# One output tile moved across the chunk border, and two product steps set next to each other, in the expert loop of an attention, experts and tanh-shrink kernel

## The chip, the cores and the metric

The kernel runs on one core of a Trainium2 chip. The metric is device time in microseconds of one execution; the median of several executions counts, and the profile shows one further execution with every instruction in time. TensorE (PE) multiplies and writes PSUM, its weight loads (PEld) are listed apart; VectorE (DVE) and ScalarE (ACT) read PSUM and write SBUF; GpSimd (POOL) works on SBUF; SyncE (SP) issues most of the DMAs.

## What is computed

```python
def _attn_ref(q, k, v, p):                  # batch 4, heads 8, seq 576, head_dim 64, 32 packed rows
    p_packed = sm_attn(p, k, v)             # softmax attention of the packed rows
    return sm_attn(q, p_packed, p_packed)   # and of all tokens over the packed rows

x = attn_out.transpose(0, 2, 1, 3).reshape(2304, 512)
p = domain_probs / (domain_probs.sum(-1, keepdims=True) + 1e-09)
for e in range(4):                          # experts, w1[e] 512x1024, w2[e] 1024x512
    h = np.maximum(x @ w1[e], 0.0)
    out += p[:, e:e + 1] * (h @ w2[e])
h = out @ w_in                              # 512x2048
return (h - np.tanh(h)) @ w_out             # 2048x512
```

## The kernel before, in words

The program has three parts: attention (to about 95 us), the expert loop (to about 650 us) and the tanh-shrink layers (to the end). The change lies in the expert loop.

The tokens are worked in two halves (`p` = 0 and 1), each of two batch elements of 576 tokens (1152 tokens, nine tiles of 128). The four experts' hidden columns are cut into eight chunks `c` of 512. For one half and one chunk the loop does these things, each named by a letter in a string of tokens that `run` reads in order:

- `g` (`up_prod`, L660): the first layer of one batch element. It is a fast block multiplication with seven products in four steps, `g<c><p><element><step>`. Steps 0 to 2 have two products of six matmuls with 288 columns each, into the PSUM tiles X and Z; step 3 has one, into X. Matmuls go on accumulating into X and Z over the steps, and between them the other engines read the intermediate sums: `kept` (ACT copies a sum out) and `done` (L686: DVE adds a kept sum to the one in PSUM at L687, then `split_h`, L610, writes the relu of it as a high part by ACT, L612, and a low part by DVE, L613). In step 2 `done` reads X first, then Z. In step 3 X gets its last product and is split.
- `d` (`down`, L723): the second layer for one tile of 128 tokens, 12 matmuls of 512 columns into a PSUM tile `yps` (two buffers), which DVE then adds to the output tile `x2` with the expert's probability (L746). Tiles 0 to 3 hold the first element only, tile 4 both, tiles 5 to 8 the second.
- `y` and `p` (`pack_pair`, `pack_held`): the next chunk's packed weights, 32 short matmuls into `wps` and the sums that the block multiplication needs (`pack_sums`, L584: four ACT and seven DVE operations).
- `a` (`stage`): loads of the next chunk's weights; `b` (`prep`): their split into high and low parts, done in the first half only and reloaded in the second; `k` (`save_w2`): storing the split ones.
- `_` (`background`, L971): one step of decoding the last layers' weights from 64-bit words, spread over DVE, ACT, POOL and DMAs. Its instructions are queued behind the last recorded DVE and ACT instruction of the steps before (`last`).

The loop runs a pair of strings per chunk: EVEN (the first element's products, with the tiles 4 to 8 of the chunk ahead) and ODD (the second element's products, with the tiles 0 to 3 of this chunk). EVEN0 and ODD0 are the same with fewer background calls; they serve the chunks 3 to 6 of the first half. The first chunks and the turn between the halves have strings of their own, as has the last chunk of the second half. So the pair of strings runs 12 times (L1091, L1092), eight times as ODD and four as ODD0.

PE and SP take their instructions in the order in which the strings issue them. DVE and ACT are ordered by a planner, which simulates the program and takes what is ready. A PSUM tile that a matmul wants to write while another engine still has to read it makes the matmul's weight load wait on a semaphore.

The order on PE around the place in question, before: g03, y, d7, d8 (both of the chunk ahead), g10, d0, g11, d1, g12, d2, g13, d3, and then the next chunk's g00. X and Z (`hpx`, `hpz`) and the first tile of `y` share two PSUM buffers of one pool.

Of the kernel before, what the change touches and what calls it, by code (L numbers as in the profile page):

```python
# [80 lines left out]
)  # L81

ODD = (
    "g%(c)d%(p)d10 a1%(e)d0 _ d%(c)d%(p)d0 _ g%(c)d%(p)d11 b%(e)d0 _ d%(c)d%(p)d1 a1%(e)d1 _ g%(c)d%(p)d12 "
    "d%(c)d%(p)d2 g%(c)d%(p)d13 p%(e)d%(q)d _ d%(c)d%(p)d3 b%(e)d1 _ "
)

EVEN0 = (
# [2 lines left out]
)  # L91

ODD0 = (
    "g%(c)d%(p)d10 a1%(e)d0 _ d%(c)d%(p)d0 _ g%(c)d%(p)d11 b%(e)d0 d%(c)d%(p)d1 a1%(e)d1 _ g%(c)d%(p)d12 "
    "d%(c)d%(p)d2 g%(c)d%(p)d13 p%(e)d%(q)d d%(c)d%(p)d3 b%(e)d1 _ "
)

LASTA = (
# [1238 lines left out]
```

## Time and profile before

| | |
|---|---|
| median of 3 runs | 1053.56 us (1053.47 to 1054.77) |
| the profiled execution | 1053.99 us, of it 1052.2 us span |
| PE busy | 1043.1 us (99%) |
| PE weight loads busy | 897.9 us (85%) |
| DVE busy | 883.1 us (84%) |
| ACT busy | 622.6 us (59%) |
| POOL busy | 162.1 us (15%) |
| granted PE clock | full speed in all slices |

The span is the time from the first to the last instruction in the profile; the execution's own time is a little longer. Matmuls overlap in the pipeline, so the durations of single ones add up to more than the time; distances between starts are the better measure. The end of a group of matmuls is read here as the start of the next matmul. "Idle before" in brackets is the idle time of an engine ahead of the instruction, and what ended it.

### The profile page before, as it was taken

To read this page: it belongs to the slowest core of one execution; us is meant where nothing else is said; L and a number is where in the kernel's file an instruction comes from. 1 tells how busy PE (TensorE), PEld (TensorE's weight loads), DVE (VectorE), ACT (ScalarE), POOL (GpSimd) and SP (SyncE) were. 2 spreads that over 40 slices of the span, in tenths; PEclk is the share of its full clock that TensorE was granted. 3 is DMA by queue.
4 is the path that set the end of the run, shared out by engine and by line. 5 is a ranking of instruction groups with operands and counts; after the bars stand their busy time and mean duration, and the time that the engine had idled before them with its cause. 6 is when DMAs were issued, how large, how long until landed. Compare 5 with 4: busy or idle time off the path is not lost.

```text
span 1052.2 us, 16516 instructions
## 1 busy us (share of the span) xinstructions
PE 1043.1 (99%) x6347; PEld 897.9 (85%) x6347; DVE 883.1 (84%) x1355; ACT 622.6 (59%) x986; POOL 162.1 (15%) x134
## 2 busy tenths in 40 slices
PE   8999999999999999999999999999999999999998
PEld 6778888788888888888888888999899899899897
DVE  5878988988986776988897986799988899988877
ACT  4555554545454455554554544578877778777775
POOL 1000032322323202424242431000000000000000
PEclk9999999999999999999999999999999999999999
DMA  9756435545654455375356254353555554564442
GB/s 337 246 188 212 171 127 187 190 161 160 220 197 134 160 175 167 139 250 180 107 205 243 83 215 164 137 214 142 195 219 186 205 202 143 205 259 162 189 170 81
DMA packets 57871, 192.75 MB, mean 183 GB/s; under 512 B 6464, under 2 KB 9024, under 8 KB 54720
## 3 DMA queue, kind: packets, MB, share of 16 engines
q1 hardware_dynamic: 57504, 191.49, 51.3%
q8 instruction: 50, 0.82, 0.3%
q14 instruction: 29, 0.24, 0.1%
q10 hardware_dynamic: 288, 0.20, 0.1%
HBM read 144.74 MB, written 46.92 MB: 182 GB/s over the span
## 4 chain that ended last, share of the span: by engine, by line
PE 96%; DVE 2%; ACT 1%; DMA 1%; issue 0%; SPq 0%; DVEq 0%
PE yps L733 37%; PE ops L1156 19%; PE h3ps L927 17%; PE hpx L676 8%; PE hpz L676 6%; PE wps L578 3%; PE hps L628 2%; PE pv L313 1%; PE qsc L335 1%; PE sc L252 1%; DMA kt<-in_kT_dram 1%; PE xps L842 0%; PE qtp L392 0%; PE tp L295 0%; PE xps L802 0%
## 5 line engine op out<-in xcount | busy, mean ns | idle before, releaser
L1156 PE MATMUL ops<-wo,gh 128*128 128x512 f32 x574 | 177.6, 390 | 0.0
L1156 PEld LDWEIGHTS ops<-wo,gh 128*128 128x128 f32 x574 | 107.1, 188 | 20.5
L746 DVE SCALAR_TENSOR_TENSOR x<-yps,pn,x 128x512 f32<-128x512 f32 x126 | 93.9, 746 | 31.2 <-PE yps L733 30.5
L733 PE MATMUL yps<-w2h,h0h 128*128 128x512 f32 x288 | 115.8, 402 | 0.0
L733 PE MATMUL yps<-w2h,h0l 128*128 128x512 f32 x288 | 113.4, 394 | 0.1
L733 PE MATMUL yps<-w2h,h1h 128*128 128x512 f32 x288 | 113.1, 393 | 0.0
L733 PE MATMUL yps<-w2l,h0h 128*128 128x512 f32 x288 | 112.9, 392 | 0.0
L1156 PE MATMUL ops<-wo,gl 128*128 128x512 f32 x287 | 112.6, 392 | 0.0
L733 PE MATMUL yps<-w2h,h1l 128*128 128x512 f32 x288 | 112.5, 391 | 0.0
L733 PE MATMUL yps<-w2l,h1h 128*128 128x512 f32 x288 | 112.2, 389 | 0.0
L927 PE MATMUL h3ps<-xh,wg 128*128 128x384 f32 x384 | 103.6, 336 | 0.0
L937 ACT ACTIVATE h<-h3ps 128x384 f32<-128x384 f32 x96 | 46.9, 490 | 70.6 <-PE h3ps L927 70.6
L449 POOL TENSOR_TENSOR fo<-fo,f 128x512 f32<-128x512 f32 x32 | 43.6, 1364 | 271.9 <-DVE f L445 184.4
L676 PE MATMUL hpx<-th,wp 128*128 128x288 f32 x336 | 80.7, 295 | 0.0
L733 PEld LDWEIGHTS yps<-w2h,h0h 128*128 128x128 f32 x288 | 54.0, 187 | 20.8 <-issue 10.9
L927 PEld LDWEIGHTS h3ps<-xh,wg 128*128 128x128 f32 x384 | 69.9, 188 | 0.7
L943 DVE TENSOR_TENSOR h<-h3ps,h 128x384 f32<-128x384 f32 x72 | 39.9, 554 | 30.6 <-PE h3ps L927 26.2
L733 PEld LDWEIGHTS yps<-w2h,h0l 128*128 128x128 f32 x288 | 54.0, 188 | 12.8 <-DVE h0l L613 0.6
L733 PEld LDWEIGHTS yps<-w2h,h1l 128*128 128x128 f32 x288 | 54.1, 188 | 12.3
L733 PEld LDWEIGHTS yps<-w2l,h1h 128*128 128x128 f32 x288 | 54.1, 188 | 12.1
L927 PE MATMUL h3ps<-xl,wg 128*128 128x384 f32 x192 | 64.3, 335 | 0.0
L733 PEld LDWEIGHTS yps<-w2h,h1h 128*128 128x128 f32 x288 | 54.1, 188 | 11.6
(192 smaller groups left out, 2591.0 us busy)
## 6 DMA issues: line engine op xcount, KB each, us to landing
wg<-wing SPq DMA_DIRECT2D x24, 1792.0 KB, 7.4
wraw<-in_w_dram SPq DMA_DIRECT2D x48, 512.0 KB, 6.4
wo<-wout SPq DMA_DIRECT2D x48, 512.0 KB, 8.7
w2s<-w2h SPq DMA_DIRECT2D x16, 512.0 KB, 3.9
w2s<-w2l SPq DMA_DIRECT2D x16, 512.0 KB, 4.3
f<-in_win_dram SPq DMA_DIRECT2D x16, 512.0 KB, 5.6
f<-in_wout_dram SPq DMA_DIRECT2D x16, 512.0 KB, 4.3
wing<-f SPq DMA_DIRECT2D x32, 256.0 KB, 4.5
```

The source lines that it names most:

```text
L252: nc.tensor.matmul(out=sc[64 * jj:64 * jj + 64, h, 0:288], lhsT=pbd[:, 4 * b + j, :], rhs=kv_k[b][j][:, 288 * h:288 * h + 288],)
L313: nc.tensor.matmul(out=pv[64 * h:64 * h + 64, jj, :], lhsT=kv_v[b][c][:, 128 * j + 64 * h:128 * j + 64 * h + 64], rhs=a1t[:, c, k0:k0 + 32 ...
L449: nc.gpsimd.tensor_tensor(out=lf, in0=lf, in1=st[:, :, 1].bitcast(F32), op=ALU.mult)
L578: nc.tensor.matmul(out=ps[32 * j:32 * j + 32, r, :], lhsT=ppbd[p][d, bi, j, 32 * r:32 * r + 32], rhs=raw[0, c, j // 2][d, j % 2, :],)
L628: nc.tensor.matmul(out=ps[:, ff, 0:n], lhsT=a[c, p, bi][:, g, c0:c0 + 128], rhs=x[p][:, g, t0:t0 + n], start=(k == 0), stop=(k == 5),)
L676: nc.tensor.matmul(out=ps[:, ff, 0:HB], lhsT=W[a][:, slot, c0], rhs=x[b], start=(start and k == 0), stop=(stop and k == 2), skip_group_che ...
L733: nc.tensor.matmul(out=ps, lhsT=a[:, ff, o:o + 128], rhs=w[c, fp][:, ff], start=(k == 0), stop=(k == 11),)
L746: last[0] = nc.vector.scalar_tensor_tensor(out=x2[tt], in0=ps, scalar=pn[:, tt, e:e + 1], in1=x2[tt], op0=ALU.mult, op1=ALU.add,).ins
L927: nc.tensor.matmul(out=ps, lhsT=wg[n][:, a, slot, 128 * kk:128 * kk + 128], rhs=x[c][b][kk] if isinstance(x[c][b], list) else x[c][b][:, k ...
L937: nc.scalar.activation(out=hs[n][a][b], in_=xz[n]["XZ".index(i)], func=ACTF.Copy)
L943: nc.vector.tensor_tensor(out=t, in0=xz[n]["XZ".index(i)], in1=t, op=ALU.add)
L1156: nc.tensor.matmul(out=ps, lhsT=a, rhs=wo[n][ff][:, w], start=(i == 0 and ff == 0 and k == 0), stop=(i == NG - 1 and ff == 1 and k == 2), ...
```

## The change

Only the two strings ODD and ODD0 are changed; no instruction is added or removed. d0 (the first output tile of this chunk) moves ahead of g10, next to d8 (the last one of the chunk ahead). g12 moves behind d2, so that g12 and g13 (third and fourth product steps of the second element) are next to each other. d1 comes between g10 and g11 and d2 between g11 and g12. The background calls keep their number and shift by a place: the first now stands ahead of d0, and of the later ones in ODD one more stands ahead of g11.

```diff
 ODD = (
-    "g%(c)d%(p)d10 a1%(e)d0 _ d%(c)d%(p)d0 _ g%(c)d%(p)d11 b%(e)d0 _ d%(c)d%(p)d1 a1%(e)d1 _ g%(c)d%(p)d12 "
-    "d%(c)d%(p)d2 g%(c)d%(p)d13 p%(e)d%(q)d _ d%(c)d%(p)d3 b%(e)d1 _ "
+    "_ d%(c)d%(p)d0 g%(c)d%(p)d10 a1%(e)d0 _ d%(c)d%(p)d1 _ g%(c)d%(p)d11 b%(e)d0 a1%(e)d1 _ "
+    "d%(c)d%(p)d2 g%(c)d%(p)d12 g%(c)d%(p)d13 p%(e)d%(q)d _ d%(c)d%(p)d3 b%(e)d1 _ "
 )
...
 ODD0 = (
-    "g%(c)d%(p)d10 a1%(e)d0 _ d%(c)d%(p)d0 _ g%(c)d%(p)d11 b%(e)d0 d%(c)d%(p)d1 a1%(e)d1 _ g%(c)d%(p)d12 "
-    "d%(c)d%(p)d2 g%(c)d%(p)d13 p%(e)d%(q)d d%(c)d%(p)d3 b%(e)d1 _ "
+    "_ d%(c)d%(p)d0 g%(c)d%(p)d10 a1%(e)d0 d%(c)d%(p)d1 _ g%(c)d%(p)d11 b%(e)d0 a1%(e)d1 _ "
+    "d%(c)d%(p)d2 g%(c)d%(p)d12 g%(c)d%(p)d13 p%(e)d%(q)d d%(c)d%(p)d3 b%(e)d1 _ "
 )
```

The order on PE after it: g03, y, d7, d8, d0, g10, d1, g11, d2, g12, g13, d3, then g00.

## Rows read from the trace of the kernel before

**Rows 1.** The page, busy us (share of the span) and instructions of each engine.
```profile
PE 1043.1 (99%) x6347; PEld 897.9 (85%) x6347; DVE 883.1 (84%) x1355; ACT 622.6 (59%) x986; POOL 162.1 (15%) x134
```

**Rows 2.** The page, the chain that ended last, share of span by engine.
```profile
PE 96%; DVE 2%; ACT 1%; DMA 1%; issue 0%; SPq 0%; DVEq 0%
```

**Rows 3.** Stretches: length, then busy us (instructions) by engine, granted clock, DMA share, GB/s.
```profile
133.45:171.45 38.00, 38.00 (x233) 31.91 (x225) 33.61 (x53) 19.45 (x33) 13.41 (x10) 1.00 0.51 160
200.00:215.00 15.00, 13.60 (x91) 10.33 (x90) 14.01 (x20) 6.82 (x12) 7.62 (x5) 1.00 0.44 141
```

**Rows 4.** The chain in order of time, merged: start us, us, what.
```profile
518.50 5.68 PE yps L733 x24
525.76 2.77 PE yps L733 x12
...
556.50 5.68 PE yps L733 x24
...
614.02 5.48 PE yps L733 x24
```

**Rows 5.** Waits of PE, whole span: us in total, times, longest.
```profile
PE wps L578 <- DVE u L687: 1.4, 1, 1.4
...
PE hps L628 <- DVE a2l L396: 0.2, 1, 0.2
```

**Rows 6.** Timeline of PE at 209: start us, us, instruction, idle before.
```profile
209.04 0.66 PE L578 MATMUL wps<-wraw,ppbd 64*32 64x512 f32 x8 [1.40 <-DVE u L687]
```

**Rows 7.** Timeline at 600: accumulation of d7, first matmul behind d8.
```profile
599.51 0.74 DVE L746 SCALAR_TENSOR_TENSOR x<-yps,pn,x 128x512 f32<-128x512 f32 x1
...
600.02 0.29 PE L676 MATMUL hpx<-a2h,wp 128*128 128x288 f32 x1
```

**Rows 8.** Timeline of PE, chunk at 518: g12's last into X, d2, g13.
```profile
533.39 0.29 PE L676 MATMUL hpx<-th,wp 128*128 128x288 f32 x1
...
534.32 0.39 PE L733 MATMUL yps<-w2h,h0h 128*128 128x512 f32 x1
...
537.06 0.29 PE L676 MATMUL hpx<-th,wp 128*128 128x288 f32 x1
```

**Rows 9.** Line L687 by form: duration ns min/median/max, first and last start.
```profile
L687 DVE TENSOR_TENSOR p<-hpx,p x28: 740/750/758, 92.1 to 646.3; 128x576 f32<-128x576 f32 x28
```

**Rows 10.** Timeline of DVE, add to X of g12 in four chunks.
```profile
150.39 0.74 DVE L687 TENSOR_TENSOR p<-hpx,p 128x576 f32<-128x576 f32 x1
...
226.19 0.76 DVE L687 TENSOR_TENSOR p<-hpx,p 128x576 f32<-128x576 f32 x1
...
571.79 0.76 DVE L687 TENSOR_TENSOR p<-hpx,p 128x576 f32<-128x576 f32 x1
...
610.54 0.75 DVE L687 TENSOR_TENSOR p<-hpx,p 128x576 f32<-128x576 f32 x1
```

**Rows 11.** Timeline of PE, first matmul behind g12 in the same chunks.
```profile
149.33 0.39 PE L733 MATMUL yps<-w2h,h0h 128*128 128x512 f32 x1
...
226.79 0.39 PE L733 MATMUL yps<-w2h,h0h 128*128 128x512 f32 x1
...
572.32 0.39 PE L733 MATMUL yps<-w2h,h0h 128*128 128x512 f32 x1
...
610.32 0.39 PE L733 MATMUL yps<-w2h,h0h 128*128 128x512 f32 x1
```

**Rows 12.** Timeline of DVE and PE at 48: a split, and the matmuls behind it.
```profile
47.82 0.76 DVE L613 SCALAR_TENSOR_TENSOR h0l<-hps,h0h 128x640 fp32r<-128x640 f32 x1
...
48.63 0.50 PE L733 MATMUL yps<-w2h,h0l 128*128 128x512 f32 x1
...
48.97 0.39 PE L733 MATMUL yps<-w2h,h0h 128*128 128x512 f32 x1
```

**Rows 13.** Timeline of DVE, chunk at 518: decoding, and the split of g13.
```profile
531.61 1.59 DVE L441 SCALAR_TENSOR_TENSOR f<-f 128x512 f32<-128x512 f32 x1 [0.41 <-ACT f L436]
...
539.35 0.74 DVE L613 SCALAR_TENSOR_TENSOR h1l<-hpx,h1h 128x576 fp32r<-128x576 f32 x1
```

## The prediction

> **What bounds the kernel now.** I read the page's busy times first, then its chain of waits, then single stretches. TensorE (PE) is busy 1043.1 us, 99% of the span [rows 1]; the chain that ended last is PE for 96% [rows 2]. So only PE time counts: an engine that finishes earlier gives nothing, and a wait on PE is paid in full unless PE waits less elsewhere. The change touches the expert loop, 12 chunk executions between 133 and 632 us: ODD0 for chunks 3 to 6 of the first half (p = 0), ODD for its chunks 2 and 7 and for chunks 1 to 6 of the second half. The stretches show how little room there is: in the first of these chunks PE is busy 38.00 of 38.00 us [rows 3], and the pair of output tiles d7, d8 comes back after exactly 38.00 us (518.50, 556.50) [rows 4]. By the waits of the whole trace PE waited for another engine seven times (longest and shortest in [rows 5]), 4.9 us in all, and one of these lies in the loop: 1.4 us, before the packed weights `wps` at 209.04 [rows 6]. That is all that a reordering of the loop could win by removing waits. The reader is to see that the loop before has no slack to win and that DVE, 33.61 of 38.00 us busy in that chunk [rows 3], is the engine that could make PE wait.
>
> **Part 1: d0 moves ahead of g10.** No matmul is added or removed: each d keeps 12 matmuls, about 2.77 us [rows 4]. Three output tiles d7, d8, d0 now follow each other. The pair d7, d8 takes 5.68 us because `wps` stands ahead of it; a pair with a product step ahead takes 5.48, so 2.74 us a tile against 2.77 [rows 4]. So d0 may gain 0.03 us in 12 chunks: 0.4 us, my only gain.
>
> What d0 needs: the high and low halves of `h` from g03, which lies the packed pair and two tiles (5.68 us for the tiles alone [rows 4]) earlier, cover enough; and an accumulator. `yps` has two buffers, so d0 takes that of d7 and waits for the DVE accumulation of d7 (L746). Before, g10 (12 matmuls of 0.13 us, 1.6 us, by the seven in 0.93 us of [rows 8]) stood between as well; now only d8 covers it. In the worst of the 12 chunks that accumulation runs from 599.51 to 600.25, and d8 ends (the next product starts) at 600.02 [rows 7]: 0.23 us late, and with the price of an exposed wait (below, 0.16) it costs 0.39 us. In three of the 12 it would end at or past d8's end, in nine before it. I take 0.7 us for the three, bounds 0 (the planner sets it ahead of other DVE work) and 3 us (a 0.25 us wait in each chunk).
>
> The weight and source loads (`a`) keep their place behind g10 and g11, so nothing there waits longer on the SP queue except behind one background call that now precedes a10; these loads are for the next chunk, 38 us away. The number of background calls is unchanged (six in ODD, four in ODD0). `b0` (a DVE subtraction and an ACT copy, in the first half only) stands behind g11 as before, one tile ahead of g12. All of this I cost at nothing; a background call that lands badly is in the bounds of part 2.
>
> **Part 2: g12 and g13 next to each other.** g12 first multiplies into X (6 matmuls), DVE then adds the kept product to X (L687, first of the two adds), and g13 goes on accumulating into the same X. So g13's first weight load waits until that add has read X. Before, d2 (2.7 us) and g12's six matmuls into Z cover the add; now only the six into Z do.
>
> Step by step, in the chunk at 518: X's last matmul starts at 533.39, Z ends (the next matmul starts) at 534.32, 0.93 us later, and g13 starts at 537.06 [rows 8]. In the new order g13 would want to start at Z's end. When does the add end? Its duration is nearly fixed, 740 to 758 ns in all 28 of this form [rows 9]; what varies is its start. With DVE free it starts 0.33 us after X's last matmul: it runs from 226.19 to 226.95, with Z's end at 226.79, so it is 0.16 us late [rows 10, 11]. With just the accumulation of the tile ahead in front of it, as d2's will be now, it ends 0.23 us late (572.55 against 572.32). With background decoding or the split of `b0` in front, 0.97 us (611.29, the last chunk) and 1.80 us (151.13, the first chunk and the worst) [rows 10, 11]. Over the 12 chunks, of which these are four, the first and the last among them, the mean is 0.80 us. In none does the add end before Z does.
>
> To this lateness comes the price of a wait that is not hidden. At 48.58 DVE ends a split (47.82 + 0.76), the waiting matmul starts at 48.63, 0.05 us later, and the next one follows 0.34 us later, where 2.77 / 12 = 0.23 is usual [rows 4]: the weight load that waits keeps the next ones from being loaded ahead. 0.05 + 0.11 = 0.16 us [rows 12].
>
> So each chunk pays at least 0.16 + 0.16 = 0.32 us and by the mean of before 0.80 + 0.16 = 0.96 us; over 12, 3.9 and 11.5 us. In the new order d2 lies between the last background call and g12, which gives DVE 2.7 us more to empty its queue, so I go below the mean of before, nearer to the 0.23 row than to 0.80: lateness 0.45 us. Term: 12 x (0.45 + 0.16) = 7.3 us.
>
> What comes after g13 has cover left: the next chunk's g00 needs X's bank of g13 for its second product, which starts g13, d3 and six matmuls (0.8 + 2.8 + 0.8 us) after g13's start; in the chunk at 518 the split of g13 ends at 540.09, 3.0 us after that start [rows 8, 13]. Cost nothing; if the cover were gone it would again be some 0.3 us a chunk.
>
> **Two rules weighed.** When PE waited at 209.04, nothing else ran on it for 1.40 us, the tiles behind it included [rows 6]. The Trainium skill (TensorE: Matmul & The Clock Gate, Step-by-step: what each phase is for) says that PE pulls only weight loads ahead and starts matmuls in program order; by that d3 cannot fill the gap behind g13 and the term stays at 7.3, whereas an engine that let d3 overtake would make it 0. The trace agrees.
>
> DVE's decode operation L441 takes 1.59 us at 531.61, and the add waits behind it, while the add itself is never stretched [rows 9, 13]. The Trainium skill (SBUF — State Buffer, SBUF: two separate sides) says that a DVE operation with two SBUF inputs and a GpSimd operation reading SBUF exclude each other. By that, splits and decoding in front of the add can double while the add, with one input in PSUM, cannot: the lateness keeps its 0.16 floor and grows a tail. The trace agrees.
>
> **Sum.** 7.3 + 0.7 - 0.4 = 7.6 us. The profiled execution of before has a span of 1052.2 us and took 1053.99 us, 0.43 above the median 1053.56. On it the sum gives 1061.6, against the median 1061.2, which I forecast.
>
> **Rivals.** (a) Cover suffices almost: every add runs at the 0.32 us floor (3.9 us), d0 never waits, the 0.4 us gain comes, and the 1.4 us wait at 209.04 vanishes by luck of the new DVE order: +2.1 us, 1055.7. For it: DVE's queue gets 2.7 us more. Against: the mean lateness today is five times the floor's 0.16. Chance 0.09. (b) Faster: d0 ahead of g10 gives DVE 2.7 us more to empty the PSUM buffer of `wps`, which g10's second product takes, and the queue behind it runs ahead far enough that PE never waits in the loop: the 1.4 us wait goes and the 0.4 us comes, 1051.8. It decides only if the add ends before Z does; start delay and duration (0.33 + 0.75 us against 0.93) speak against that. Chance 0.04. (c) Slower by more: the background calls land in front of the add as now (0.96 us a chunk, 11.5 us), and d0 waits too (1 to 3 us): 1066 to 1068 us. For it: DVE is near 88% busy and its splits stretch. Chance 0.15. (d) The change does not do what it says, the wait moves onto another instruction and costs nothing: inside (a). The forecast, +4 to +11 us, has 0.72.
>
> **How the numbers follow.** A measurement of this kernel can tell about 0.2% (2.1 us) from no change. Slower by more: 0.72 + 0.15, a little less for a forecast that lands at its edge, 0.86. Within: 0.10. Faster: 0.04. The range 1056.0 to 1066.5 runs from just above (a) to the lower end of (c) and leaves out about 2 in 10. The clock is no term: the granted clock stayed at 1.00 (2.4 GHz) through the stretch with the 1.40 us gap [rows 3].
>
> **What would show it.** After: waits of PE (or its weight loads) on L687 in `hpx`, about 12, 0.3 to 1.9 us each, sum near 6 us; chunks of 38.3 to 39.5 us in place of 38.00; g13's second matmul 0.24 us behind its first. Against it: no such waits, chunks still at 38.00, or d0 waiting on L746 for more than g13 does on L687. Wrong most easily: the DVE order, which a planner sets and I don't know.

## The result, and the profile after

The median went from 1053.56 to 1063.54 us (five runs each: 1052.96 to 1054.77 and 1062.6 to 1064.33). The ratio is 1.0089 with a 95% interval of 1.0077 to 1.0100: slower by 0.89%, 10.0 us. The profiled execution of after took 1062.79 us with a span of 1061.0, 8.8 us more than that of before; the sum of the prediction was 7.6, its forecast 1061.2 and its range 1056.0 to 1066.5. The loop, from the first d7 to the first matmul of the last layers, grew from 527.22 to 536.36 us (+9.14); ahead of it and behind it nothing grew (-0.29 and -0.05). The page of after, to compare with [rows 1]:

```profile
PE 1046.8 (99%) x6347; PEld 898.2 (85%) x6347; DVE 874.9 (82%) x1355; ACT 622.2 (59%) x986; POOL 160.6 (15%) x134
```

PE executes the same matmuls, yet its busy time grew by 3.7 us, not 0: "busy 99%" hides short waits, because the ends of matmuls, which the profile models, run over the small gaps. The waits of after (all of the span: us in total, times, longest), against [rows 5], show more, above all on the weight loads (PEld):

```profile
PE hpx L676 <- DVE p L687: 5.1, 6, 2.5
PE wps L578 <- DVE u L687: 1.4, 1, 1.4
...
PEld hpx L676 <- DVE p L687: 8.4, 12, 2.7
...
PEld yps L733 <- DVE x L746: 0.9, 2, 0.6
```

There are the 12 new waits of g13 on the add L687, and two of d0 on the accumulation of d7. The old wait for `wps` is still there [rows 6]. On PE itself the profile counts only six of the twelve; the other six are so short that they show on the weight loads alone. The start of one of these, in the chunk at 410 (timeline: start us, us, instruction):

```profile
427.45 0.75 DVE L746 SCALAR_TENSOR_TENSOR x<-yps,pn,x 128x512 f32<-128x512 f32 x1 [0.32 <-PE yps L733]
428.24 0.76 DVE L687 TENSOR_TENSOR p<-hpx,p 128x576 f32<-128x576 f32 x1
...
428.70 0.29 PE L676 MATMUL hpz<-a2h,wp 128*128 128x288 f32 x1
429.05 0.40 PE L676 MATMUL hpx<-th,wp 128*128 128x288 f32 x1
429.29 0.30 PE L676 MATMUL hpx<-tl,wp 128*128 128x288 f32 x1
```

The add stands behind nothing but d2's accumulation and ends at 429.00. g13's first matmul starts 0.05 us later, 0.35 behind the last one into Z where 0.13 is usual: 0.22 lost. The second follows 0.24 behind the first, again 0.11 more than usual. I call the first kind the gap in front of g13; the floor of a wait is 0.22 + 0.11 = 0.33 us. The same reading in all 12 chunks gives these gaps, in their order: first half 0.41, 1.09, 0.22, 0.79, 0.47, 2.68 (sum 5.66), second half 0.22, 0.29, 0.60, 0.29, 0.29, 0.22 (sum 1.91). With 12 x 0.107 in front of the second matmul that is 8.86 us. d0's two waits cost 0.58, and d7, d8, d0 in a row take 8.31 us, 0.05 less a chunk than two and one took before [rows 4], 0.6 in all. 8.86 + 0.58 - 0.6 = 8.84 us, of the 9.14 by which the loop grew. The rest is mostly d2: it takes 2.77 us ahead of g12 (424.48 to 427.25 in the chunk above) where it took 2.74 ahead of g13 [rows 8], 0.36 us in 12 chunks. With it the account of the profiled execution closes to 0.1 us.

One chunk as a whole, against the 38.00 of [rows 3], and the 4 us behind the longest wait (length, then busy us and instructions of PE, PEld, DVE, ACT and POOL, granted clock, DMA share, GB/s):

```profile
410.23:448.51 38.28, 38.22 (x232) 31.88 (x224) 30.64 (x47) 20.14 (x35) 13.47 (x11) 1.00 0.45 165
...
350.00:354.00 4.00, 4.00 (x20) 3.32 (x19) 3.97 (x6) 3.07 (x5) 0.85 (x1) 1.00 0.00 0
```

Why the gaps of the first half are longer, its timeline shows. In the second of the 12 chunks the split of the weights (`b0`, L551) and two operations of decoding (L426, L430) stand ahead of the add:

```profile
187.78 1.22 DVE L551 TENSOR_TENSOR w2l<-wraw,w2h 128x1024 fp32r<-128x1024 f32 x1 [1.47 <-ACT w2h L547]
188.93 0.42 DVE L426 TENSOR_SCALAR f<-f 128x512 uint32<-128x512 uint32 x1
189.26 0.74 DVE L746 SCALAR_TENSOR_TENSOR x<-yps,pn,x 128x512 f32<-128x512 f32 x1
189.92 0.68 DVE L430 SCALAR_TENSOR_TENSOR f<-f 128x512 uint32<-128x512 uint32 x1
190.52 0.75 DVE L687 TENSOR_TENSOR p<-hpx,p 128x576 f32<-128x576 f32 x1
...
191.33 0.40 PE L676 MATMUL hpx<-th,wp 128*128 128x288 f32 x1 [0.93 <-DVE p L687]
```

The longest wait, in the last chunk of the first half, has a cause that I had not looked for. There each output tile is also stored (L751). Since d0 now precedes a10, its store stands ahead of a10's reloads on the SP queue (SPq), and the fetch of the next words to decode (L418) behind both:

```profile
337.23 0.32 SPq L751 DMA_DIRECT2D xs<-x  x1
337.64 1.51 SPq L529 DMA_DIRECT2D w2h<-w2s  x1
...
339.68 0.42 SPq L418 DMA_DIRECT2D f<-in_win_dram  x1
...
346.12 0.66 ACT L425 ACTIVATE fo<-f 128x512 f32<-128x512 uint32 x1 [2.50 <-DMA f<-in_win_dram]
...
346.81 0.43 DVE L426 TENSOR_SCALAR f<-f 128x512 uint32<-128x512 uint32 x1 [4.84 <-ACT fo L425]
347.15 0.74 DVE L746 SCALAR_TENSOR_TENSOR x<-yps,pn,x 128x512 f32<-128x512 f32 x1
347.81 0.68 DVE L430 SCALAR_TENSOR_TENSOR f<-f 128x512 uint32<-128x512 uint32 x1
348.41 0.75 DVE L687 TENSOR_TENSOR p<-hpx,p 128x576 f32<-128x576 f32 x1
...
349.22 0.41 PE L676 MATMUL hpx<-th,wp 128*128 128x288 f32 x1 [2.52 <-DVE p L687]
```

ACT waits for the fetch, DVE stands idle for 4.84 us at L426, and the accumulation of d2 and the add are ordered behind it. The same place in the kernel before, where the planner had set the same L426 behind both adds:

```profile
340.25 0.76 DVE L687 TENSOR_TENSOR p<-hpx,p 128x576 f32<-128x576 f32 x1
...
342.84 1.34 DVE L426 TENSOR_SCALAR f<-f 128x512 uint32<-128x512 uint32 x1
```

### The profile page after: what moved, and what is told of

It is laid out like the page before. It is cut to its first block, busy times and chain, and to the rows that moved or that the text cites. A ratio compares the mean times of both kernels' runs of the same rounds, so it can differ in the third digit from the quotient of the medians.

```text
span 1061.0 us, 16512 instructions
## 1 busy us (share of the span) xinstructions
PE 1046.8 (99%) x6347; PEld 898.2 (85%) x6347; DVE 874.9 (82%) x1355; ACT 622.2 (59%) x986; POOL 160.6 (15%) x134
## 5 line engine op out<-in xcount | busy, mean ns | idle before, releaser
L676 PEld LDWEIGHTS hpx<-th,wp 128*128 128x128 f32 x336 | 58.6, 188 | 11.2 <-DVE p L687 8.4
```

The costliest lines, as they stand in the source:

```text
L676: nc.tensor.matmul(out=ps[:, ff, 0:HB], lhsT=W[a][:, slot, c0], rhs=x[b], start=(start and k == 0), stop=(stop and k == 2), skip_group_che ...
```

## The experiments

The diffs show the tokens of ODD without the marks for chunk, half and element (`g12` is step 2 of the second element); ODD0 is changed alike. Each time is compared with the kernel before on the same chip.

**The two parts alone.** The first experiment leaves d0 where it was and makes part 2 alone:

```diff
-g10 a10 _ d0 _ g11 b0 _ d1 a11 _ g12 d2 g13 p _ d3 b1 _
+g10 a10 _ d0 _ g11 b0 _ d1 a11 _ d2 g12 g13 p _ d3 b1 _
```

> Part 2 alone: d0 stays behind g10, g12 moves behind d2 next to g13, background calls where they were. Theory (g13 waits for the DVE add that reads X): 12 waits on L687 in front of g13, 0.3 to 2.7 us each, +8 to +10 us against the kernel before (1061.5 to 1063.5). Rival 1 (the loss comes from d0's move, through the accumulator of d7 or the shifted background calls): within 1.5 us of before, no such waits.

Measured: 1056.23 against 1053.72 us, ratio 1.0022 [1.0013, 1.0031], +2.5 us. The expectation was far too high. Its waits of weight loads, and the place of g13 in the third of the 12 chunks (timeline: start us, us, instruction):

```profile
PEld hpx L676 <- DVE p L687: 4.5, 13, 0.9
```

```profile
227.22 0.75 DVE L746 SCALAR_TENSOR_TENSOR x<-yps,pn,x 128x512 f32<-128x512 f32 x1 [1.92 <-PE yps L733]
228.01 0.76 DVE L687 TENSOR_TENSOR p<-hpx,p 128x576 f32<-128x576 f32 x1
...
228.47 0.29 PE L676 MATMUL hpz<-a2h,wp 128*128 128x288 f32 x1
228.82 0.40 PE L676 MATMUL hpx<-th,wp 128*128 128x288 f32 x1
```

The waits are there (12 of the 13 are g13's), but nearly all at the floor: nothing but d2's accumulation stands in front of the add, and in the chunk shown DVE has been idle for 1.92 us when d2 ends. The gaps sum to 1.96 in the first half and 1.46 in the second, with the second matmuls (12 x 0.106) to 4.7 us, and the `wps` wait of 1.5 is gone by luck: 3.2 net. So a g13 next to g12 is not dear by itself; what made it dear in after is something that part 1 brings.

The other part alone: d0 moved, but the add covered, by cutting d3 in two (`h3`: its first six matmuls, `j3`: the rest). The first of two kernels does this alone:

```diff
-_ d0 g10 a10 _ d1 _ g11 b0 a11 _ d2 g12 g13 p _ d3 b1 _
+_ d0 g10 a10 _ d1 _ g11 b0 a11 _ d2 g12 h3 g13 p _ j3 b1 _
```

> The changed kernel with d3 cut in two: its first six matmuls stand between g12 and g13, the other six behind g13. Theory: 1.4 us more cover; of the 12 waits of the changed kernel only one was longer than that (2.7 us), so -0.5 to +2.5 us against before (1053 to 1056). Rival 1 (d0's move): it stays at +8 to +10 us. Rival 2 (any shorter distance between g12 and g00 costs, so the wait moves on to g00, which has only six matmuls of d3 in front now): the waits appear in front of g00's second product, +3 us or more.

Measured: 1058.24 us, ratio 1.0037 [1.0024, 1.0049], missed: +4.5. Of the 12 waits one is left, in the last chunk of the first half (1.5 us with its second matmul); a new one of 0.4 us stands in front of g03 of a later chunk. But d0's weight loads wait for the accumulation of d7 four times, up to 1.5 us of PE time, and `wps` waits twice. The second kernel also puts a10's reloads back ahead of d0's store:

```diff
-_ d0 g10 a10 _ d1 _ g11 b0 a11 _ d2 g12 h3 g13 p _ j3 b1 _
+a10 _ d0 g10 _ d1 _ g11 b0 a11 _ d2 g12 h3 g13 p _ j3 b1 _
```

> The kernel with half of d3 between g12 and g13 (1058.2) and a10 ahead of d0. It keeps d0's place and takes the add's cover as before, so what is left is the price of d0's move. Theory: the 1.4 us wait in front of g13 in chunk 7 of the first half goes, d0's waits on the accumulation of d7 (L746, 2.5 us in three chunks) stay, 1056 to 1057. Rival 1: 1058 as without it.

Measured: 1056.70 against 1054.37, ratio 1.0027 [1.0017, 1.0037], +2.3 us, as expected. Its waits of weight loads:

```profile
PEld yps L733 <- DVE x L746: 3.3, 4, 1.8
...
PEld hpx L676 <- DVE p L687: 1.3, 2, 0.7
```

One of the two waits on L687 is g13's, the other the one in front of g03. This is the price of d0's place with the add covered. The two parts apart cost 2.5 and 2.3 to 4.5 us, together 10.0: they are not additive. Of the 5.2 us missing from 2.5 + 2.3, some 1.5 us is the `wps` wait that the first experiment lost by luck, the rest the first half's gaps, 5.66 in after against 1.96 there.

**After with one thing changed: the store on SP.** If the store in front of the reloads makes the longest wait, a10 ahead of d0 should take it away:

```diff
-_ d0 g10 a10 _ d1 _ g11 b0 a11 _ d2 g12 g13 p _ d3 b1 _
+a10 _ d0 g10 _ d1 _ g11 b0 a11 _ d2 g12 g13 p _ d3 b1 _
```

> The changed kernel with a10 (loads of the next chunk's weights) ahead of d0, so that SP has issued them before it comes to d0's store. In chunk 7 of the first half d0 also stores its output (L751); in the changed kernel that store stands on SP ahead of a10 and of the fetch for the decoding, which is issued at 339.68, 2.5 us behind the store, lands at 346.1, and DVE's decoding operation L426, planned ahead of the tile's accumulation and the add, waits for it: the longest of the 12 waits, 2.7 us. Theory (SP's order): that wait falls to 0.3 to 1 us, the others stay; -1.5 to -2.5 us on the changed kernel, +7.5 to +8.5 us against before (1061 to 1062). Rival 1 (the fetch is late for another reason): the 2.7 us wait and +9 to +10 us stay.

Measured: 1063.00 us, ratio 1.0084 [1.0070, 1.0098], not to be told from after; missed. In that chunk:

```profile
338.36 0.32 SPq L751 DMA_DIRECT2D xs<-x  x1
338.73 0.42 SPq L418 DMA_DIRECT2D f<-in_win_dram  x1
...
345.34 1.07 DVE L426 TENSOR_SCALAR f<-f 128x512 uint32<-128x512 uint32 x1 [2.23 <-ACT fo L425]
346.45 1.69 DVE L430 SCALAR_TENSOR_TENSOR f<-f 128x512 uint32<-128x512 uint32 x1
...
348.72 0.74 DVE L687 TENSOR_TENSOR p<-hpx,p 128x576 f32<-128x576 f32 x1
...
349.52 0.40 PE L676 MATMUL hpx<-th,wp 128*128 128x288 f32 x1 [1.68 <-DVE p L687]
```

The fetch is issued 0.4 us behind the store instead of 2.5, and the gap shrinks from 2.68 to 1.84 us; DVE still takes the decoding ahead of the add, and both its operations are now stretched (1.07 and 1.69 against 0.43 and 0.68). The other eleven gaps stay within 0.02 us of those of after. So the SP queue is worth 0.8 us of this wait, shown; the order of DVE keeps the rest.

**The work in front of the add.** Two edits of after move it. All background calls but one behind p:

```diff
-_ d0 g10 a10 _ d1 _ g11 b0 a11 _ d2 g12 g13 p _ d3 b1 _
+d0 g10 a10 d1 g11 b0 a11 d2 g12 g13 p _ _ _ _ _ d3 b1 _
```

> The changed kernel with all but the last background call of ODD and ODD0 moved behind g13 and p. Theory with two terms (floor of the add plus what is queued before it on DVE): without decoding work before it the add is 0.16 to 0.23 us late in most chunks, so a wait costs 0.3 to 0.4 us, 12 of them 4 to 5 us, total +4 to +6 us against before (1057.5 to 1059.5). Rival 3 (the queue has no part, the wait is the add's own latency): +9 to +10 us as in the changed kernel. Rival 4 (the decoding work has to go somewhere and now delays g13's split): waits in front of g00, +6 us or more in all.

Measured: 1083.88 us, ratio 1.0276 [1.0260, 1.0292], missed by far. g13's gaps in that order are 0.22 to 0.29 us each, the floor, although `b0` stands where it was; but the heaped decoding meets d7's accumulation of the next chunk, and d0 pays:

```profile
PE yps L733 <- DVE x L746: 11.6, 6, 2.4
```

So without decoding in front of the add there are no long gaps, and taken from there it costs more elsewhere. `b0` alone behind p:

```diff
-... g11 b0 a11 _ d2 g12 g13 p _ d3 b1 _
+... g11 a11 _ d2 g12 g13 p b0 _ d3 b1 _
```

> The changed kernel with b0 (the DVE subtraction and ACT copy that split the next chunk's weights, first half only) moved from behind g11 to behind g13 and p. In the changed kernel the first six waits in front of g13 (p = 0, where b0 does work) add up to 5.7 us before the exposed 0.1 us each, the six of the second half to 1.9 us; with only the steps adjacent it was 2.0 and 1.5. Theory (the part above the floor comes from b0, which lies one tile ahead of g12 in the changed kernel and two tiles ahead there): waits of the first half fall to 2 us, total +5 to +7 us against before (1058.7 to 1060.7). Rival 1 (it comes from d0's move and the shifted background calls): +9 to +10 us as in the changed kernel. Rival 2 (the split comes back behind g13, where the packed sums are): new waits elsewhere, +8 us or more.

Measured: 1068.59 us, ratio 1.0137 [1.0119, 1.0155], missed. In the first half's five chunks without a store the gaps fall from 2.98 to 1.38 us, 0.22 to 0.29 each; the sixth, with the store, stays at 2.59. So the gaps of these five are long only where `b0` and decoding both stand between g11 and the add: with either of them taken away, all five are at the floor. But the products of the next chunk now wait, as its waits of weight loads show:

```profile
PEld hpx L676 <- DVE p L687: 9.1, 14, 2.7
...
PEld hpz L676 <- DVE p L687: 3.6, 5, 1.7
```

Not all of the time is theirs: three of the four runs have a mean granted clock of 0.997 or 0.998 and took 1067.81 to 1069.51 us, the fourth, at 1.00, took 1064.36 (the last section returns to this).

A third edit, on part 2 alone, tests whether the distance from `b0` to g12 is the point. It moves `b0` a tile nearer:

```diff
-g10 a10 _ d0 _ g11 b0 _ d1 a11 _ d2 g12 g13 p _ d3 b1 _
+g10 a10 _ d0 _ g11 _ d1 b0 a11 _ d2 g12 g13 p _ d3 b1 _
```

> Part 2 alone (1056.2), with b0 behind d1 instead of ahead of it, so that it lies one tile ahead of g12, as in the changed kernel; d0 and the loads stay where they were before the change. With part 2 alone the waits in front of g13 are 2.0 us in the six chunks of the first half and 1.5 us in those of the second, without the exposed 0.1 us each; in the changed kernel 5.7 and 1.9 us. Theory (the difference comes from the split of b0 and the decoding behind it, one tile ahead of the add, not from d0's place): 4 to 5.5 us in the first half, 1.5 us in the second; +2 to +3.5 us on part 2 alone, 1058 to 1060. Rival 1 (d0's place among the tiles or SP's order does it): waits and time as with part 2 alone, 1055.5 to 1057.

Measured: 1058.83 against 1053.44, ratio 1.0051 [1.0038, 1.0065]; a time inside the expectation, but for other reasons. The first half's gaps came to 2.5 us, not 4 to 5.5; most of the 2.9 us between it and the first experiment is the `wps` wait of 1.5, which is back:

```profile
PEld hpx L676 <- DVE p L687: 4.9, 12, 0.9
...
PEld wps L578 <- DVE u L687: 1.7, 1, 1.7
```

`b0`'s nearness in the string is therefore a small part. What is left is an argument that fits after and these runs and was not tried by itself: in the first experiment two tiles, 5.5 us of PE, lie between g11 and g12, in after one, 2.7 us, as in the kernel before. ACT's copies of g11 come first, then the decoding and `b0` that queue behind them, and DVE needs these 2.7 us more to be done when g12 ends. With d0 out of the gaps between g10, g11 and g12, only d1 and d2 are left for them.

**The wait by itself.** What covers the add, and what does not. Three edits put other work around it. On part 2 alone, Z's product ahead of X's in g12 takes its cover away:

```diff
-            mul(X, 5, cmb(2), False, False)
-            done(X, p5, 1, 1)
-            mul(Z, 6, tok(1, 1), False, True)
-            done(Z, u, 0, 1)
+            for k in ("XZ", "ZX")[bi]:
+                mul(*((X, 5, cmb(2), False, False) if k == "X" else (Z, 6, tok(1, 1), False, True)))
+                done(*((X, p5, 1, 1) if k == "X" else (Z, u, 0, 1)))
```

> As part 2 alone (1056.2), with g12's two products of the second element changed about: Z first, then X, so that nothing lies between X's last matmul and g13. Theory (g13 waits for start delay and duration of the add, 0.33 + 0.75 us, of which Z's six matmuls hid 0.79): each of 12 waits grows by 0.8 us, +9.5 us on part 2 alone, 1065 to 1067. Rival 1 (the wait is not on this add): 1056 to 1057.

Measured: 1069.09 us, ratio 1.0148 [1.0135, 1.0162].

```profile
231.02 0.30 PE L676 MATMUL hpx<-th,wp 128*128 128x288 f32 x1
...
231.35 0.76 DVE L687 TENSOR_TENSOR p<-hpx,p 128x576 f32<-128x576 f32 x1
...
232.17 0.40 PE L676 MATMUL hpx<-th,wp 128*128 128x288 f32 x1 [0.85 <-DVE p L687]
```

The gap is 1.02 us in place of 0.22, in nearly every chunk: the six matmuls of 0.13 us lost as cover. 12 such chunks make 9.6 us, but the time is 15.7 above before, 13.2 more than part 2 alone and some 2 more than expected: the `wps` wait of 1.4 us is back, and the clock fell behind one gap (last section). The add starts 0.33 us behind X's last matmul, takes 0.76, and g13 starts 0.06 later. Those three numbers, less the matmuls left between, make the floor. On part 2 alone again, half of d2 between g12 and g13 (`h2`, `j2` as above) removes the wait:

```diff
-g10 a10 _ d0 _ g11 b0 _ d1 a11 _ d2 g12 g13 p _ d3 b1 _
+g10 a10 _ d0 _ g11 b0 _ d1 a11 _ h2 g12 j2 g13 p _ d3 b1 _
```

> The kernel with part 2 alone (1056.2) with d2 cut in two: six matmuls ahead of g12, six between g12 and g13, d0 and the background calls where they were before. Theory (the floor of 0.33 us a chunk needs 0.3 us of cover, and half a tile is 1.4): 11 or 12 waits in front of g13 vanish, -4 to -5 us on part 2 alone: 1051.2 to 1052.5, -1 to -2 us against before, the 1.5 us wait at the packed weights staying away as in part 2 alone. Rival 1 (the DVE order changes again and other waits come): 1053 to 1057.

Measured: 1054.04 against 1054.37, ratio 1.0001 [0.9992, 1.0010]. All 12 waits are gone, but the gain of 1 to 2 us on before did not come: `wps` waits as there, and in the profiled execution, which at 1055.97 us was the slowest of eleven, another wait came, for a load.

```profile
PE wps L578 <- DMA wraw<-in_w_dram: 1.5, 1, 1.5
PE wps L578 <- DVE u L687: 1.4, 1, 1.4
```

This is the fastest order tried, and no faster than before.

A whole tile between, with d3 put there in after, moves the wait on:

```diff
-_ d0 g10 a10 _ d1 _ g11 b0 a11 _ d2 g12 g13 p _ d3 b1 _
+_ d0 g10 a10 _ d1 _ g11 b0 a11 _ d2 g12 d3 g13 p _ b1 _
```

> The changed kernel with d3 between g12 and g13, so that nothing but g00's first product stands between g13 and the product that takes its PSUM buffer. Theory (five gaps, four tiles to cover them): the waits in front of g13 vanish and come back in front of g00's second product, which needs the split of g13: before, that split ended 1.8 to 2.7 us behind g13's last matmul, and the six matmuls in between cover 0.9, so 1.0 to 1.9 us a chunk with the exposed wait, +12 to +20 us against before. Rival 5 (g13's split has cover enough): no waits, -0.5 to +1.5 us.

Measured: 1068.49 us, ratio 1.0134 [1.0120, 1.0148]. Now g13 stands next to the next chunk's g00, whose second product waits for the split of g13 in ten chunks:

```profile
PEld hpz L676 <- DVE h1l L613: 9.7, 10, 1.0
```

The pair of kernels with the add cut into two halves of 288 columns, on part 2 alone and on the kernel with `b0` behind p, was to start g13 on the first half while DVE adds the second:

```diff
-            nc.vector.tensor_tensor(out=t, in0=ps[:, :, 0:HB], in1=t, op=ALU.add)
+            for k in range(2) if (bi, fp) == (1, 1) else [slice(2)]: nc.vector.tensor_tensor(out=t[:, k], in0=ps[:, k, 0:HB], in1=t[:, k], op=ALU.add)
```

> As the kernel with part 2 alone (1056.2), but the add of g12 that reads X is two DVE instructions, one for each PSUM bank, 288 columns each. g13 writes the first bank first, so its first matmul needs the first add only, which can start 0.4 us earlier and is 0.33 us shorter. Theory (the floor is the add's own end, 0.16 to 0.23 us late): 11 of 12 waits vanish, -4 us against part 2 alone, 1051.5 to 1053, so -0.5 to -2 us against before. Rival 1 (the wait is on the tile, not on the bank, or the two adds cost DVE as much as they save): 1056 to 1057.

> The changed kernel with b0 behind g13 (as in the run before it) and the add in two halves. Theory: what is left are d0's two waits (0.6 us), the 1.5 us wait at the packed weights if it stays, and now and then a late add, less 0.6 us for three tiles in a row: 0 to +2 us against before (1053.7 to 1055.7). Rival 1: no better than the run with b0 alone moved.

Measured: 1059.41 us, 1.0055 [1.0041, 1.0069], and 1067.01 us, 1.0124 [1.0109, 1.0139]; both missed. The first is slower than part 2 alone; the second cannot be told from the kernel with `b0` behind p, and as there the one run at a granted clock of 1.00 is the fastest (1063.67 us). In the first:

```profile
229.97 0.82 DVE L687 TENSOR_TENSOR p<-hpx,p 128x288 f32<-128x288 f32 x2
...
230.85 0.40 PE L676 MATMUL hpx<-th,wp 128*128 128x288 f32 x1
```

The two halves run to 230.79 and g13 starts 0.06 behind the second, 0.06 later than with one add: the gap is 0.285 instead of 0.22. Why the first half does not release the first matmul these runs don't tell.

## Why the prediction was right, point by point

- **What bounds the kernel**: right. A wait on PE was paid in full; the list of waits on PE, with the gain of three tiles in a row, gives 8.84 us of the 9.14 by which the loop grew.
- **The exposed wait**, 0.05 + 0.11 us, read from one place outside the loop [rows 12]: 0.05 + 0.107. The floor, 0.32 a chunk from [rows 10, 11], is 0.33. That no add would end ahead of Z held in all 12.
- **The lateness**, 0.45 us a chunk: this term was mis-sized. It measured 7.58 / 12 - 0.05 = 0.58, so the term of 7.3 us is 8.9. The mean hides three values: 2.63 in the sixth chunk, (2.98 - 0.25) / 5 = 0.55 in the five before it, and (1.91 - 0.3) / 6 = 0.27 in the second half. In the kernel before the same three, read as for the mean of 0.80, were 0.23, 0.88 and 0.83. My reason for going below that mean, that d2 gives DVE 2.7 us more after the last background call, fits eleven chunks: their mean fell from 0.85 to 0.40, below my 0.45. What the term had wrong is the sixth alone, 2.2 us above the forecast.
- **"All of this I cost at nothing; a background call that lands badly is in the bounds of part 2"**: this is the step that failed. In the sixth chunk one landed badly, and the sum had no term for it. Its 2.63 us have two parts: L426 and L430 are planned ahead of the add, where before both stood behind it, and the fetch for them is late, 0.8 us. Of `b0` the sentence was right as far as it went: `b0` and g11 stand one tile ahead of g12 before and after, and the five chunks in question became less late, not more. But `b0` is not free: with it away their gaps lose 1.6 us in all.
- **"Nothing there waits longer on the SP queue except behind one background call"**: this failed, and is this 0.8 us. Of the moved d0 I counted the matmuls and the accumulation, not the store that it issues in one chunk.
- **d0 waits for d7's accumulation**, 0.7 us, bounds 0 to 3: 0.58, in two chunks. The worst of before [rows 7] was the right row: the longest took 0.41. **The gain** of 0.4 us was 0.6, of which d2, now ahead of g12, gave 0.36 back. **g13 to g00** covered: right in after; the cover is d3, and the kernel without it paid 9.7 us there.
- **The clock is no term**: too simple. The stretch behind the longest wait kept 1.00, as its row shows, but two of the five runs of after have a mean granted clock of 0.998 and took 1063.78 and 1064.33, the three at 1.00 between 1062.60 and 1063.54. Of the 2.3 us by which the forecast lies below the median, 1.2 are the sum's (8.8 against 7.6), the lateness above all; the other 1.2 lie between the profiled executions and the medians, 0.43 above that of before and 0.75 below that of after.
- **Rivals**: (a), all at the floor and the `wps` wait gone, is close to what part 2 alone does, +2.5 us against my +2.1; with d0's move it did not come. (b) never came: the order without any of the 12 waits is no faster than before. (c) needed 0.96 us a chunk; the whole paid 0.74, and only the first half, by its sixth chunk, more (1.05). That the term of 7.3 us came as near as it did is in part luck: eleven chunks together cost 0.6 us less than forecast, and the sixth, not foreseen, 2.2 more.

Of the two rules weighed, the first: the Trainium skill (TensorE: Matmul & The Clock Gate, Step-by-step: what each phase is for) says that matmuls stay in program order. The trace agrees: in none of the 12 chunks did d3 fill the gap.

The second: what grows in front of the add is decoding and splits, L551 from 1.22 to 1.87 us in the fourth chunk of after and L430 from 0.68 to 1.69 in the kernel with the loads first, both while GpSimd worked (L450 from 346.08 to 347.58 there), and the add stayed at 0.74 to 0.76. The Trainium skill (SBUF — State Buffer, SBUF: two separate sides) says that a DVE operation with two SBUF inputs and a GpSimd operation that reads SBUF exclude each other. The trace agrees for these; L426, which has one SBUF input, was stretched too (0.43 to 1.07), and that the two inputs do not explain.

## What to carry to other kernels

When two steps that accumulate into one tile, with a read between, come next to each other, set start delay plus duration of the read against the matmuls left between (here 0.33 + 0.76 against 0.93): a shortfall is paid each time with the exposed weight load on top, and half an output tile between took the wait away in 12 and in 11 of 12 chunks. What a moved tile leaves behind counts as much as where it goes: by the argument above, which was not tried by itself, d0's move took away the time in which DVE emptied its queue, and two moves that cost 2.3 to 4.5 us each cost 10 together. Follow every instruction that a moved step issues, in its special chunks too.

## What the runs showed of the hardware

The granted clock fell to half, 1.2 GHz, behind some long gaps on PE. In the kernel with the background calls behind p, PE started no matmul between 296.08 and 298.88. The stretches ahead of the gap, with it, and behind it (columns as above):

```profile
290.00:296.00 6.00, 6.00 (x39) 4.38 (x24) 6.00 (x8) 2.24 (x6) 2.02 (x2) 1.00 0.45 133
296.00:299.00 3.00, 0.58 (x4) 0.16 (x3) 2.68 (x7) 1.06 (x2) 2.57 (x2) 1.00 0.00 0
299.40:303.10 3.70, 3.70 (x11) 2.84 (x10) 1.78 (x2) 0.00 (x0) 0.00 (x0) 0.54 0.36 76
303.10:308.00 4.90, 4.90 (x29) 4.37 (x28) 2.42 (x4) 1.34 (x2) 0.00 (x0) 1.00 0.93 347
```

From 299.45 to 303.10 there are nine distances of matmuls of one tile, 0.43 us most of them where 0.23 is usual: 3.65 - 9 x 0.23 = 1.6 us on top of the gap. The kernel with `b0` behind p shows 0.50 for 3.2 us behind a gap of 2.73 us, the one with Z first 0.52 for 3.1 us behind one of 2.25. After had a gap of 2.81 us (346.41 to 349.22) and kept 1.00 in the profiled execution. So such a gap is sometimes paid more than once; what decides it, the runs don't show.
